# Four more w_out tiles summed on TensorE, and a newly searched order, in an attention-plus-FFN kernel

## The chip, the cores and the metric

The kernel runs on one core of a Trainium2 chip. The metric is the device time of one launch in microseconds; three runs of the kernel before gave a median of 753.57 us. Engines are called PE (TensorE matmul, PEld its weight loads), DVE (VectorE), ACT (ScalarE), POOL (GpSimd) and SP (SyncE, which issues most DMAs).

## The reference

Block-causal attention over 8 batches, 8 heads, 576 positions and 64 channels per head (blocks of 64 positions), whose output is the input of a gated feed-forward layer. The weights `w_in`, `conv_w` and `w_out` arrive as float64.

```python
scores = q @ k.T / 8;  scores[block_i < block_j] = -1e9
x = softmax(scores) @ v                      # (8, 576, 512) over heads
h = maximum(x @ w_in, 0)                     # 512 -> 1024
conv_out[t] = sum_k conv_w[k] * h[t + k - 1] # 3 taps along the sequence
out = (h * sigmoid(conv_out)) @ w_out        # 1024 -> 512
```

## The kernel before

Matmuls run in fp32r, and precision is kept by splitting each operand in a high part and a low part (`hi`, `lo`), so that a product is three matmuls: in L1872 `wih`x`x`, `wil`x`x` and `wih`x`x` low (x @ w_in), and in L1938 `woh`x`gh`, `wol`x`gh`, `woh`x`gl` (the second product of the layer). A pair of heads is a visit: scores (L1475, L1477, L1428), maximum and exponential (L1485, L1488), normalizing on POOL (L1399), transposes (L1670), product with v (L1790). The first batch is done in two parts, A (positions 0 to 255, lines L1331, L1583, L1609, L1766) and B (the rest, lines L1522, L1541, L1424), so that the feed-forward work starts early. After every fourth visit `ffn` adds two halves of the feed-forward layer of a batch.

The weights are decoded from float64 during the first batch, in 16 tiles of 128 x 512 numbers: `load_w_in` for tiles f = 0 to 7 (through the buffers `gh`, `gl`, named by tile parity) and `load_w_out` for f = 8 to 15 (raw words in `x`, scratch in `stage`). Both call `split`, whose steps are: a DMA (L1147 or L1173); `decode` with ACT Abs (L1018), a clamp (L1024, on POOL for every tile but the first), three DVE integer steps (L1029, L1041, L1045) and a DVE product that gives the remainder of the word (L1052). Then there are two ways:

- Where f is not in `WPE` (`whole`), POOL adds the remainder to the main part (L1056), ACT rounds that to `hi` (L1087), and POOL subtracts `hi` to give `lo` (L1090).
- Where f is in `WPE`, ACT rounds the main part to `hi`, DVE writes the remainder into `lo`, PE forms `lo` minus `hi` in a PSUM bank with two 512-column matmuls (L1103 with `nident`, L1106 with `rident`), and DVE adds the main part and writes `lo` (L1109).

The order of the instructions is not that of the code. Each step is recorded with an engine, a guessed duration, its dependences and buffers, and `Plan.order` lays them out: from the numbers in `TARGETS` (one due time for each step) and the guessed durations it simulates the five engines and writes out each engine's queue. The engines then run their queues strictly in that order, and wait on semaphores. The planner puts filler matmuls (L2090, on `blank` or `rident`, 512 columns, result unused) into PE's queue wherever its own simulation leaves PE idle for more than 0.4 us; how many, comes out of its guess. For DMAs it keeps one running time `moved` for the transfers: each transfer begins at the later of `moved` and 1.2 us after its issue, and takes `xfer`, times 1.5 as long as `moved` is under a limit.

Of the kernel before, what the change touches and what calls it, by code (L numbers as in the profile page):

```python
# [18 lines left out]
PE, DVE, ACT, POOL, SP = 0, 1, 2, 3, 4  # L19

TARGETS = """
# [299 lines left out]
class Plan:  # L321
# [53 lines left out]
    def order(self, targets, skip, fill, clock, pair):  # L375
# [76 lines left out]
        moved = 0.0  # L452
        done = []
        left = len(self.ops)
        while left:
            left -= 1
            best = None
            for e in range(5):
                t = free[e]
                if e == PE:  # L460
# [3 lines left out]
                    for o in open_:  # L464
                        at, need = vacant(o, t)
# [4 lines left out]
                        at = max(at, rtime[o.seq])  # L470
# [1656 lines left out]
```

## Time and profile before

| | |
|---|---|
| median of 3 runs | 753.57 us (753.52 to 753.73) |
| the profiled execution | 753.84 us, its span 752.1 us |
| PE busy | 743.1 us, 5169 matmuls |
| DVE, ACT, POOL busy | 623.4, 603.7, 435.9 us |
| granted TensorE clock | 1.000 |

The span runs from the first to the last instruction; the 1.7 us beside it lie around the program. A busy PE is not PE at its peak: an isolated matmul also counts for the time in which its weights are loaded and its result drains, and the filler matmuls count too. "idle before" is the time in which the engine had nothing to do ahead of a group of instructions, and what ended that. The chain is the sequence of work that ended last, followed back from the last instruction.

### The profile page before, as it was taken

How to read it: one execution, taken by the hardware profiler on the slowest of the kernel's cores; microseconds unless marked ns; L12 is line 12 of the kernel's file. 1: busy time of each engine (PE TensorE's matmuls, PEld its weight loads, DVE VectorE, ACT ScalarE, POOL GpSimd, SP SyncE). 2: the span in 40 equal slices, each digit the busy share in tenths (PEclk: the TensorE clock that was granted, in tenths of full speed). 3: DMA queues.
4: the chain of work that ended last, by engine and by line, in shares of the span. 5: the costliest groups of instructions: out<-in, count | busy, mean ns of one | idle time of the engine just before them, and what ended most of it. 6: DMA issues, size and time to landing. Idle time of an engine off the chain costs nothing.

```text
span 752.1 us, 16813 instructions
## 1 busy us (share of the span) xinstructions
PE 743.1 (99%) x5169; PEld 668.6 (89%) x5169; DVE 623.4 (83%) x1836; ACT 603.7 (80%) x1754; POOL 435.9 (58%) x650
## 2 busy tenths in 40 slices
PE   8999999999999999999999999999999999999998
PEld 5567899889899898999989899998989889898997
DVE  6998999999989698898979789898988779896541
ACT  5989989778988687887979679797978769786752
POOL 2557678656666457475665547566566555565421
PEclk9999999999999999999999999999999999999999
DMA  9763857566553546655462655544565445430001
GB/s 264 183 167 104 192 119 165 120 158 158 129 135 91 132 106 145 145 125 134 102 149 70 158 130 128 142 107 117 126 137 127 110 122 134 118 78 15 15 28 43
DMA packets 165628, 92.63 MB, mean 123 GB/s; under 512 B 134924, under 2 KB 142116, under 8 KB 165540
## 3 DMA queue, kind: packets, MB, share of 16 engines
q1 hardware_dynamic: 164996, 91.43, 50.0%
q8 instruction: 42, 0.69, 0.4%
q14 instruction: 46, 0.38, 0.2%
q10 hardware_dynamic: 544, 0.13, 0.1%
HBM read 38.30 MB, written 9.44 MB: 63 GB/s over the span
## 4 chain that ended last, share of the span: by engine, by line
PE 85%; ACT 5%; DMA 3%; DVE 3%; POOL 2%; SPq 2%; issue 1%; ACTq 0%; POOLq 0%
PE bank L1938 26%; PE bank L1872 25%; PE bank L1790 11%; PE bank L1670 7%; PE bank L1477 4%; PE bank L1475 4%; PE bank L1428 3%; PE bank L1221 2%; DMA qkf<-in_k_dram 1%; PE bank L1766 1%; DMA vn<-in_v_dram 1%; ACT p4f L1444 1%; DMA x<-in_moe_w_out_dram 1%; DMA qnf<-in_k_dram 0%; DVE st L1485 0%
## 5 line engine op out<-in xcount | busy, mean ns | idle before, releaser
L1872 PE MATMUL bank<-x,wih 128*128 128x290 f32 (+3 forms) x1024 | 199.6, 300 | 0.1
L1912 POOL TENSOR_TENSOR gl<-t,gh 128x289 fp32r<-128x289 f32 (+3 forms) x128 | 103.7, 815 | 101.7 <-ACT gh L1909 96.7
L1872 PEld LDWEIGHTS bank<-x,wih 128*128 128x128 f32 x1024 | 157.0, 189 | 3.2 <-ACT p3f L1488 0.3
L1938 PE MATMUL bank<-woh,gh 128*128 128x512 f32 (+1 forms) x296 | 118.5, 400 | 0.0
L1938 PE MATMUL bank<-wol,gh 128*128 128x512 f32 (+1 forms) x296 | 115.0, 388 | 0.0
L1938 PE MATMUL bank<-woh,gl 128*128 128x512 f32 (+1 forms) x296 | 114.9, 388 | 0.0
L1872 PE MATMUL bank<-x,wil 128*128 128x290 f32 (+3 forms) x512 | 111.1, 298 | 0.0
L1485 DVE TENSOR_REDUCE st<-bank 128x1 f32<-128x128 f32 (+1 forms) x224 | 107.3, 483 | 2.9
L1684 DVE TENSOR_TENSOR ptbl<-bank,ptbh 128x512 fp32r<-128x512 f32 (+1 forms) x142 | 89.3, 632 | 4.5 <-ACT ptbh L1681 1.9
L1681 ACT ACTIVATE ptbh<-bank 128x512 fp32r<-128x512 f32 (+2 forms) x180 | 87.4, 502 | 6.8 <-PE bank L1670 5.8
L1893 DVE SCALAR_TENSOR_TENSOR t<-bank,cw,t 128x289 f32<-128x289 f32 (+3 forms) x128 | 64.7, 505 | 23.1 <-ACT t L1889 21.3
L1872 PEld LDWEIGHTS bank<-x,wil 128*128 128x128 f32 x512 | 82.3, 188 | 0.6
L840 POOL TENSOR_SCALAR vv<-vn 128x320 fp32r<-128x320 f32 (+2 forms) x62 | 28.0, 453 | 88.1 <-PE bank L1790 37.0
L1477 PE MATMUL bank<-kl,qz 128*128 128x128 f32 (+1 forms) x224 | 71.7, 322 | 0.0
L1938 PEld LDWEIGHTS bank<-woh,gl 128*128 128x128 f32 x296 | 55.5, 188 | 12.6
L1889 ACT ACTIVATE t<-bank,cw 128x289 f32<-128x289 f32 (+3 forms) x128 | 64.2, 502 | 2.3
L1897 DVE SCALAR_TENSOR_TENSOR t<-bank,cw,t 128x288 f32<-128x288 f32 (+3 forms) x128 | 64.7, 506 | 1.1
L1813 DVE TENSOR_TENSOR xt<-bank,xt 64x256 f32<-64x256 f32 x112 | 51.5, 460 | 16.0 <-ACT xt L1810 13.0
L1790 PE MATMUL bank<-ptbl,vv 128*64 128x192 f32 x240 | 64.6, 314 | 0.0
L1902 ACT ACTIVATE t<-t 128x289 f32<-128x289 f32 (+3 forms) x128 | 56.9, 445 | 7.0 <-DVE t L1897 6.1
L1909 ACT ACTIVATE gh<-t 128x289 fp32r<-128x289 f32 (+3 forms) x128 | 56.1, 444 | 7.4 <-DVE t L1905 6.7
L1905 DVE SCALAR_TENSOR_TENSOR t<-t,bank 128x289 f32<-128x289 f32 (+3 forms) x128 | 57.0, 447 | 5.0 <-ACT t L1902 4.1
(186 smaller groups left out, 2009.2 us busy)
## 6 DMA issues: line engine op xcount, KB each, us to landing
out_dram<-stage SPq DMA_DIRECT2D x35, 256.0 KB, 2.2
ka<-kh SPq DMA_DIRECT2D x56, 144.0 KB, 2.6
kb<-kh SPq DMA_DIRECT2D x56, 144.0 KB, 2.6
vn<-in_v_dram SPq DMA_DIRECT2D x60, 128.0 KB, 2.7
qnf<-in_q_dram SPq DMA_DIRECT2D x56, 128.0 KB, 2.4
knf<-in_k_dram SPq DMA_DIRECT2D x56, 128.0 KB, 2.7
x<-in_moe_w_out_dram SPq DMA_DIRECT2D x8, 512.0 KB, 4.8
qz<-qh SPq DMA_DIRECT2D x28, 144.0 KB, 2.5
```

Source lines behind the costliest of these rows:

```text
L1477: nc.tensor.matmul(sb.ap[:, 0:nk], qz.ap[:, z:z + 128], kl.ap[:, 0:nk], start=False, stop=True)
L1485: nc.vector.tensor_reduce(out=st.ap[:, i:i + 1], in_=sb.ap[:, 0:nk], op=ALU.max, axis=AX.X, negate=True)
L1681: nc.scalar.activation(out=hi(), in_=src(), func=AF.Copy)
L1684: nc.vector.tensor_tensor(out=lo(), in0=src(), in1=hi(), op=ALU.subtract)
L1790: nc.tensor.matmul(tb.ap[0:m, q0 - qa:qb - qa], vv.ap[:, chunk(c), w[ps_]], pm.ap[:, 128 * c + q0:128 * c + qb] if qa == 0 else pm.ap[:, c ...
L1872: nc.tensor.matmul(fb.ap[:, 0:n2], wt[:, c, fs], xs[c][xi].ap[:, x0:x0 + n2], start=(n + c - c0 == 0), stop=(n + c - c0 == 3 * NCC - 1))
L1889: nc.scalar.activation(out=t.ap[:, 0:no], in_=fb.ap[:, own:own + no], func=AF.Copy, scale=cw[:, NFC + f:NFC + f + 1])
L1893: nc.vector.scalar_tensor_tensor(out=t.ap[:, i0:no], in0=fb.ap[:, own + i0 - 1:own + no - 1], scalar=cw[:, f:f + 1], in1=t.ap[:, i0:no], o ...
L1897: nc.vector.scalar_tensor_tensor(out=t.ap[:, 0:i1], in0=fb.ap[:, own + 1:own + 1 + i1], scalar=cw[:, 2 * NFC + f:2 * NFC + f + 1], in1=t.a ...
L1905: nc.vector.scalar_tensor_tensor(out=t.ap[:, 0:no], in0=t.ap[:, 0:no], scalar=1.0, in1=fb.ap[:, own:own + no], op0=ALU.add, op1=ALU.mult)
L1912: nc.gpsimd.tensor_tensor(out=gbuf[1].ap[:, f, carry:carry + no], in0=t.ap[:, 0:no], in1=gbuf[0].ap[:, f, carry:carry + no], op=ALU.subtract)
L1938: nc.tensor.matmul(fb.ap[:, 0:cut], gbuf[a].ap[:, f, cs], w[:, f, ds], start=(f == 0 and n == 0), stop=(f == NFC - 1 and n == 2))
```

## The change

Three things are edited. `WPE` takes in the four w_out tiles that were left out (f = 9, 11, 13, 15), so that all 16 weight tiles go the second way. The planner's price of transfers is changed in two places: the limit under which a transfer takes 1.5 times as long goes from 4.5 to 8.5 us, and the transfer of a v tile goes from 0.8 to 1.5 us. And all the numbers in `TARGETS` are others, found by a new search, so every engine's queue is in another order from the first instructions on.

```diff
 TARGETS = """
-242 286 317 355 385 418 264 296 365 340 443 409 460 486 708 703 273 378 423 422 441 482 495 520 534 541 415 421 419 426 634 594 433 456 482 496 494 483 501
...
+213 152 338 292 386 451 201 231 335 331 431 412 398 340 749 696 120 185 245 198 282 248 281 294 300 357 316 355 348 355 558 558 406 384 411 393 409 426 498
...
@@ -545,7 +545,7 @@
             if e == SP:
 
                 o.end = max(o.end, moved - 4.4)
-                moved = max(o.end + 1.2, moved) + o.xfer * (1.5 if moved < 4.5 else 1.0)
+                moved = max(o.end + 1.2, moved) + o.xfer * (1.5 if moved < 8.5 else 1.0)
                 o.lat = moved + 0.4 - o.end
@@ -652,7 +652,7 @@
     EA = True
-    WPE = tuple(range(8)) + (8, 10, 12, 14)
+    WPE = tuple(range(16))
     WPA = ()
@@ -898,7 +898,7 @@
-        ld = pl.op(SP, 2.4, go, at if load_at is None else load_at, bufs=[vn], xfer=0.8)
+        ld = pl.op(SP, 2.4, go, at if load_at is None else load_at, bufs=[vn], xfer=1.5)
```

Counted over the whole program, PE gets 8 more real matmuls of 512 columns (L1103 and L1106, 4 to 8 each on `woh` and `wol`), DVE 4 more instructions (L1109), POOL 8 fewer (4 of L1056, 4 of L1090); ACT and SP have the same instructions in another order. There are 38 fillers in both: 18 on `blank` and 20 on `rident` before, 19 and 19 now.

POOL's queue around the second w_out tile, where the first batch's scores of part B are normalized (`p2f`, `p3f`). Before:

```order
L1559 TENSOR_SCALAR p3f_105<-p3f_105,st_145 128x512
L1056 TENSOR_TENSOR stage<-stage,x 128x512
L1559 TENSOR_SCALAR p2f_99<-p2f_99,st_147 128x384
L1024 TENSOR_SCALAR stage<-stage 128x512
L1090 TENSOR_TENSOR wol<-stage,woh 128x512
L1559 TENSOR_SCALAR p2f_101<-p2f_101,st_147 128x384
L1912 TENSOR_TENSOR gl<-t,gh 128x255
```

Now:

```order
L1559 TENSOR_SCALAR p3f_105<-p3f_105,st_145 128x512
L1559 TENSOR_SCALAR p2f_99<-p2f_99,st_147 128x384
L1559 TENSOR_SCALAR p2f_101<-p2f_101,st_147 128x384
L1024 TENSOR_SCALAR stage<-stage 128x512
L1559 TENSOR_SCALAR p3f_103<-p3f_103,st_147 128x512
L1559 TENSOR_SCALAR p3f_105<-p3f_105,st_147 128x512
L1912 TENSOR_TENSOR gl<-t,gh 128x255
```

Two 512-column POOL instructions between the normalizing steps are gone, and the clamp L1024 of the tile stands behind two of those steps.

PE's queue at the last fillers, in part A of the first batch (`qkr` are q and k to be transposed, `p0r`, `p1r` the exponentials, `ptah`, `ptal` their transposes). Before, where the last filler is the one after `wih`:

```order
L2090 MATMUL bank<-rident 128x512 x4
L1766 MATMUL bank<-ptal,ptbl 64x256
L1766 MATMUL bank<-ptal,ptbl 64x128
L2090 MATMUL bank<-rident 128x512 x3
L1670 MATMUL bank<-rident,p0r_92 128x128
L1670 MATMUL bank<-rident,p1r_96 128x128 x2
L2090 MATMUL bank<-rident 128x512
...
L1103 MATMUL bank<-wih,nident 128x512
L2090 MATMUL bank<-rident 128x512
```

Now, where the last are the three ahead of `qkr_118`:

```order
L2090 MATMUL bank<-rident 128x512
L1670 MATMUL bank<-rident,p0r_94 128x128
L1670 MATMUL bank<-rident,p1r_98 128x128 x2
L1766 MATMUL bank<-ptah,ptbl 64x256
L1766 MATMUL bank<-ptah,ptbl 64x128
L1331 MATMUL bank<-rident,qkr_124 128x128 x4
L2090 MATMUL bank<-rident 128x512 x3
L1331 MATMUL bank<-rident,qkr_118 128x128 x4
```

The fillers now end earlier in the work: ahead of the last one stood 78 real matmuls before, and 45 now.

SP's queue of loads at the start (`gh`, `gl` are w_in tiles, `x` a w_out tile, `t` conv_w, `qkf` q and k of part A). Before:

```order
L1147 DMA gh_184<-in_moe_w_in_dram 128x4x256
L1147 DMA gl_186<-in_moe_w_in_dram 128x4x256
L1147 DMA gh_184<-in_moe_w_in_dram 128x2x256
L957 DMA qkf00_113<-in_q_dram 128x2x64
L1189 DMA t_191<-in_moe_conv_w_dram 24x256
...
L1147 DMA gl_186<-in_moe_w_in_dram 128x4x256
L957 DMA qkf01_115<-in_q_dram 128x2x64
```

Now:

```order
L1147 DMA gh_185<-in_moe_w_in_dram 128x4x256
L1189 DMA t_187<-in_moe_conv_w_dram 24x256
L1147 DMA gl_189<-in_moe_w_in_dram 128x4x256
L1147 DMA gh_185<-in_moe_w_in_dram 128x2x256
L957 DMA qkf00_113<-in_q_dram 128x2x64 x2
L1147 DMA gl_189<-in_moe_w_in_dram 128x4x256
L1173 DMA x_143<-in_moe_w_out_dram 128x1024
L957 DMA qkf01_115<-in_q_dram 128x2x64
```

conv_w moves to second place, and the first w_out tile comes ahead of the second pair of heads (`qkf01`), where it came in 13th place before.

434 rows, old and new, of the table TARGETS are left out of this document.

## The prediction

> **What bounds the kernel now.** I read first the page's busy times and its chain, then busy time by stretches, then the waits, and last the groups of the instructions that change.
>
> ```profile
> span 752.1 us, 16813 instructions
> PE 743.1 (99%) x5169; PEld 668.6 (89%) x5169; DVE 623.4 (83%) x1836; ACT 603.7 (80%) x1754; POOL 435.9 (58%) x650
> PE 85%; ACT 5%; DMA 3%; DVE 3%; POOL 2%; SPq 2%; issue 1%; ACTq 0%; POOLq 0%
> ```
>
> PE is busy for all but 9.0 us, and 85% of the chain is PE's. The other 15% (113 us) is where an order can win or lose. The next view (stretches of the span; columns: length, then busy us and instructions of each engine, granted clock, DMA) shows where those lie.
>
> ```profile
> 0.00:8.00 8.00, 6.89 (x18) 5.11 (x18) 1.98 (x11) 3.12 (x6) 1.70 (x8) 1.00 0.80 237
> 8.00:20.00 12.00, 10.15 (x70) 6.98 (x70) 11.58 (x34) 8.57 (x27) 4.25 (x8) 1.00 1.14 287
> 20.00:30.00 10.00, 9.19 (x57) 5.94 (x54) 9.17 (x27) 9.32 (x31) 5.49 (x9) 1.00 0.85 213
> 30.00:40.00 10.00, 9.04 (x53) 5.71 (x53) 9.50 (x23) 9.54 (x30) 4.30 (x10) 1.00 0.48 125
> 40.00:50.00 10.00, 10.00 (x73) 7.76 (x72) 9.47 (x27) 7.93 (x26) 6.21 (x7) 1.00 0.69 184
> 50.00:60.00 10.00, 9.28 (x52) 5.71 (x51) 9.23 (x25) 9.45 (x27) 6.48 (x10) 1.00 0.45 123
> 60.00:80.00 20.00, 20.00 (x147) 15.79 (x146) 16.04 (x41) 19.51 (x56) 12.40 (x20) 1.00 0.45 119
> 80.00:100.00 20.00, 19.89 (x134) 16.94 (x135) 18.71 (x53) 17.98 (x54) 15.18 (x22) 1.00 0.70 162
> 200.00:700.00 500.00, 500.00 (x3557) 462.76 (x3556) 423.31 (x1268) 405.02 (x1184) 296.94 (x445) 1.00 0.49 119
> ```
>
> From 200 us on PE never stops, and DVE has 15% to spare: there no order wins much, and any matmul added costs its full time. Up to 60 us it is otherwise. DVE and ACT are at 92 to 97% in most stretches, and PE's idle time sums, after the first 8 us, to 1.85 + 0.81 + 0.96 + 0 + 0.72 = 4.3 us. In those 60 us PE also runs its fillers, which are no work:
>
> ```profile
> L2090 PE MATMUL bank<-blank 128*128 128x512 f32 x18 | 6.9, 562 | 1.1 <-DVE blank L834 1.1
> L2090 PE MATMUL bank<-rident 128*128 128x512 f32 x20 | 6.7, 424 | 0.3 <-ACT qa L845 0.3
> ```
>
> So 13.6 us of fillers and 4.3 us of idle time stand in the first 60 us: a start that is limited by the loads and by DVE and ACT. What PE waited for there, and which waits a load ended (engine, line, what ended it: us, times, longest):
>
> ```profile
> PE bank L1103 <- ACT wih L1087: 0.8, 2, 0.5
> PE bank L1766 <- ACT ptah L845: 0.7, 2, 0.4
> PE bank L1670 <- POOL p1f L1624: 0.6, 2, 0.4
> PE bank L1424 <- ACT ptbh L845: 0.5, 1, 0.5
> ...
> ACT gh L1018 <- DMA gh<-in_moe_w_in_dram: 1.9, 1, 1.9
> ACT gl L1018 <- DMA gl<-in_moe_w_in_dram: 1.2, 1, 1.2
> ACT stage L1018 <- DMA x<-in_moe_w_out_dram: 1.2, 1, 1.2
> ```
>
> PE is held by ACT above all, and ACT by loads three times. The chain of waits shows the third one with its consequence (start, us, what), and two later places:
>
> ```profile
> 45.75 3.93 DMA x<-in_moe_w_out_dram
> 49.70 0.05 ACT stage L1018
> ...
> 53.10 0.75 PE bank L1424 x2
> ...
> 82.99 1.30 POOL stage L1056
> 84.32 0.63 ACT woh L1087
> ...
> 94.01 2.06 DMA vn<-in_v_dram
> ```
>
> ACT's queue stood until 49.7 us for a w_out tile that took 3.93 us to land, and PE's next score matmul (L1424) waited behind it. Later a POOL sum that the change removes is on the chain (1.30 us), and then a v tile (2.06 us), whose price the change raises.
>
> **The change part by part.** The groups (line, engine, operation, form, count | busy, mean ns | idle before):
>
> ```profile
> L1103 PE MATMUL bank<-woh,nident 128*128 128x512 f32 x4 | 1.7, 414 | 0.0
> L1106 PE MATMUL bank<-wol,rident 128*128 128x512 f32 x4 | 1.8, 461 | 0.1
> L1109 DVE TENSOR_TENSOR wol<-bank,stage 128x512 fp32r<-128x512 f32 x4 | 2.7, 679 | 0.0
> L1056 POOL TENSOR_TENSOR stage<-stage,x 128x512 f32<-128x512 f32 x4 | 5.2, 1305 | 5.9 <-DVE x L1052 4.0 <-DVE st L1548 1.8
> L1090 POOL TENSOR_TENSOR wol<-stage,woh 128x512 fp32r<-128x512 f32 x4 | 5.1, 1282 | 1.3 <-ACT woh L1087 1.3
> ...
> 708.15 11.20 PE bank L1938 x48
> ```
>
> *PE, eight matmuls more.* Their means of 414 and 461 ns run from issue to the modelled end and overlap their neighbours. In a stream, 48 matmuls of 512 columns took 11.20 us on the chain, 233 ns each. Eight cost 8 x 0.233 = 1.9 us. Ends: 0, if all fall into idle time of the start, and 3.5 us at the means (4 x 0.414 + 4 x 0.461). I take 1.9, since the tiles stand at 40 to 110 us, where PE is busy nearly without a break.
>
> *Fillers.* One more on `blank`, one fewer on `rident`. The extra one runs before the first decoded tile is there: the first L1103 waited for ACT behind all 18. Cost 0; if that cover were gone, 0.23.
>
> *DVE, four L1109 more.* 4 x 0.679 = 2.7 us. From 40 to 100 us DVE is idle for 0.53 + 0.77 + 3.96 + 1.29 = 6.6 us, so that there is room, and the next stage has more. I take 0; the ends are 0 and +2.7, if DVE has no gap where these fall.
>
> DVE's step on the raw w_out words may get cheaper when POOL is quieter (duration ns min/median/max):
>
> ```profile
> L1041 DVE SCALAR_TENSOR_TENSOR stage<-x,stage x8: 673/732/1007, 20.0 to 98.8; 128x512 int32<-128x512 int32 x8
> ```
>
> The Trainium skill (SBUF — State Buffer, on the shared port pair) says that a DVE operation with two SBUF inputs and a GpSimd operation that reads SBUF exclude each other, and the second to come stands still until the first is done. The spread from 673 to 1007 ns agrees with that without showing its cause. By that rule, the sum would be lower by up to 8 x (732 - 673) ns = 0.5 us of DVE's time, which is hidden like the 2.7 us.
>
> *POOL, eight fewer.* 4 x 1.305 + 4 x 1.282 = 10.3 us go from an engine that is 62 to 76% busy there. Nobody on PE waits for these by the trace; ACT's L1087 does, once on the chain. A tile of the second way needs no L1056 ahead of L1087. I take -0.4; ends 0 and -1.3, the one sum on the chain. What is late next at that place is `p4f`, which had the exponentials of part B to wait for anyway.
>
> *The new order and the new prices.* This is the largest term, and the trace of before cannot show it. The order in front of the reader has its fillers behind 45 real matmuls instead of 78: with slower loads assumed, the planner puts its empty time in the beginning and then has PE fed. The w_out tiles' loads stand further ahead of their use (the first moves past the loads of the second pair of heads, which are then later by its transfer; conv_w past two w_in tiles). The steps of the loads move past each other in SP's queue alone; POOL issues none. What such an order can win at most is the idle time and the `rident` fillers after 8 us, 4.3 + 6.7 = 11 us; what it can lose is as much idle time again, 4.3 us. I take the idle time from 20 to 60 us, 0.81 + 0.96 + 0.72 = 2.5 us, and ACT's wait for the w_out tile, 1.2 us, which it handed on to PE: -3.7. The first two ACT waits on loads stay: the first tile is still the first load. The number is nearer to the small end because DVE and ACT, at 92 to 97%, can't deliver much sooner.
>
> Sum against the profiled execution's 753.84 us: +1.9 + 0 + 0 - 0.4 - 3.7 = -2.2, 751.6 us. The median of the runs is 0.27 us below that execution, so 751.4 us.
>
> **The rivals.**
>
> *The waits only move (no change).* DVE and ACT set the pace of the start, and an order doesn't make them faster. For it: 11.58 of 12 us DVE busy at 8 to 20 us, 9.5 of 10 after that. Against it: ACT falls to 7.93 at 40 to 50 us, just where it stands for a load. Then the order wins no more than the w_out wait and the POOL sum, 1.2 + 0.4, against 1.9: 753.57 + 0.3 = 753.9 us.
>
> *DVE becomes the bound (slower).* Place: 40 to 100 us. The four L1109 lie in front of the maxima (L1538, L1431) that ACT and then PE need. Price: 2.7 us on top of PE's 1.9, with the 1.6 us of the rival above won: 753.57 + 2.7 + 1.9 - 1.6 = 756.6 us. It decides once DVE is over 95% busy in the whole stretch of 40 to 100 us; before, it had 80% at 60 to 80 us, which speaks against it.
>
> *The loads are priced too late (slower).* A filler that the planner puts in runs whether the data is there or not. The new queue has one run of eight on `rident`; if the data is there when it begins, PE loses 8 x 0.233 = 1.9 us, and with the 1.9 of the added matmuls and 1.6 won the time is 755.8 us. Against it: the start's loads took long in the trace of before too.
>
> ```profile
> 1.27 5.34 DMA qkf<-in_k_dram
> 7.04 2.66 DMA qkf<-in_q_dram
> 14.26 3.72 DMA qnf<-in_k_dram
> ```
>
> **How the numbers follow.** My forecast has 0.44, the waits that only move 0.29, DVE as the bound 0.17, loads priced too late 0.10. A measurement of this kernel can tell 0.2% (1.5 us) from no change. The first is faster by about that much and more, so faster 0.44, same 0.29, slower 0.27. The likeliest case alone spans 749.2 (753.57 + 1.9 - 0.4, less the 4.3 us of idle time after 8 us and 1.6 us of fillers) to 752.0 (where the order wins 3.1 us in place of 3.7). The range for 8 in 10 takes in the no-change case and the two slower ones: 749.0 to 756.6 us.
>
> **What would show it.** In the profile after: PE with 8 more matmuls and some 1.9 us more of work; L1109 at 8 on `wol`; L1056 and L1090 gone from the w_out tiles and POOL at about 426 us. If I am right, PE idles under 2 us from 20 to 60 us, and ACT has no wait for a w_out load over 0.5 us. If DVE is the bound, its stretches from 40 to 100 us are over 95%, and PE waits for maxima. If loads are priced too late, the run of eight fillers ends well after the landing of its q and k. What would make it wrong beside these is the late part: if PE's waits after 200 us, now 0, come to microseconds because the new order has another engine late there, or if the last tiles, which the order mixes more closely with the last x @ w_in matmuls, wait for ACT, DVE and POOL at the end.

## The result and the profile after

The changed kernel took 757.71 us (757.28 to 758.90, three runs): 4.14 us more, a ratio of 1.0055 with a 95% interval of 1.0040 to 1.0070. The prediction was 751.4 us, 749.0 to 756.6. The profiled execution took 757.71 us, its span is 755.9 us.

The page of the changed kernel, span, busy times and chain:

```profile
span 755.9 us, 16813 instructions
PE 745.6 (99%) x5177; PEld 669.5 (89%) x5177; DVE 629.5 (83%) x1840; ACT 605.3 (80%) x1754; POOL 426.8 (56%) x642
PE 85%; DVE 6%; ACT 5%; DMA 2%; issue 1%; POOL 0%; SPq 0%; ACTq 0%; DVEq 0%
```

PE has 2.5 us more of busy time and 1.3 us more outside it. On the chain POOL and SP's queue fall from 2% each to 0% and DVE doubles, from 3 to 6%. By stretches (columns as before):

```profile
0.00:8.00 8.00, 6.24 (x19) 4.69 (x19) 2.63 (x15) 3.04 (x7) 1.32 (x7) 1.00 0.75 218
8.00:20.00 12.00, 9.65 (x55) 6.51 (x56) 10.15 (x29) 7.53 (x23) 3.72 (x5) 1.00 1.01 274
20.00:30.00 10.00, 9.08 (x66) 6.10 (x65) 9.18 (x28) 8.83 (x30) 4.62 (x10) 1.00 0.86 210
30.00:40.00 10.00, 9.49 (x59) 6.15 (x59) 9.50 (x27) 9.90 (x33) 4.45 (x10) 1.00 0.45 115
40.00:50.00 10.00, 9.99 (x68) 7.26 (x69) 9.56 (x25) 9.63 (x28) 6.19 (x8) 1.00 0.55 138
50.00:60.00 10.00, 9.79 (x55) 6.22 (x54) 9.46 (x24) 7.70 (x22) 3.58 (x5) 1.00 0.70 182
60.00:80.00 20.00, 19.61 (x138) 15.43 (x137) 17.37 (x43) 19.05 (x55) 11.54 (x19) 1.00 0.38 114
80.00:100.00 20.00, 19.77 (x130) 16.30 (x130) 18.79 (x55) 18.35 (x54) 11.77 (x18) 1.00 0.74 177
200.00:700.00 500.00, 499.55 (x3546) 461.57 (x3545) 428.68 (x1277) 407.00 (x1189) 297.93 (x445) 1.00 0.50 119
```

From 20 to 60 us PE idles 0.92 + 0.51 + 0.01 + 0.21 = 1.65 us, against 2.49 before: what the prediction hoped for came. But from 0 to 20 us it idles 4.11 us instead of 2.96, and 8 to 20 us holds 55 matmuls instead of 70. The last row matters most: in the same 500 us PE runs 3546 matmuls instead of 3557, and DVE is busy for 5.4 us more, in a stretch that has none of the added instructions. DVE's instructions haven't become longer: over the whole program their durations sum to 704.8 us before and 707.5 after, and the 2.7 us are the four L1109. In the stretch, 9 more of them fall (1277 against 1268), and neighbours overlap less in the trace (sum of durations less busy time: 52.5 us before, 50.0 after).

Two waits of the first 60 us, and the groups of the change, in the changed kernel:

```profile
PE bank L1331 <- DMA qkf<-in_k_dram: 0.9, 1, 0.9
...
ACT stage L1018 <- DMA x<-in_moe_w_out_dram: 0.4, 1, 0.4
```

```profile
L1103 PE MATMUL bank<-woh,nident 128*128 128x512 f32 x8 | 3.8, 475 | 0.3 <-DVE t L1905 0.2
L1106 PE MATMUL bank<-wol,rident 128*128 128x512 f32 x8 | 3.3, 410 | 0.0
L1109 DVE TENSOR_TENSOR wol<-bank,stage 128x512 fp32r<-128x512 f32 x8 | 5.4, 679 | 0.2 <-PE bank L1106 0.2
```

PE now waits for k of part A (L1331), which it did not before; ACT's wait for a w_out tile is down from 1.2 to 0.4 us.

**Where the time is lost, by the starts of the matmuls.** "Busy" doesn't tell what a matmul's wait inside the pipeline costs, so I took every start of a PE matmul from the trace and the gap to the next start. What a gap after a matmul of a line and shape needs, I took from the kernel before: the lower quartile of such gaps (for L1331, L1424 and the matmuls of part A's and B's scores, which start in pairs, the mean). The rest is called lost; a filler's gap is lost as a whole. Needed time is 692.60 us before and 694.65 after, 2.05 us more for the eight matmuls. Lost time by stretch, in us:

| kernel | 0-20 | 20-60 | 60-200 | 200-700 |
|---|---|---|---|---|
| before | 12.38 | 10.08 | 11.45 | 20.62 |
| after | 13.80 | 8.57 | 11.24 | 22.79 |
| e1_plus8 | 12.40 | 9.58 | 10.87 | 20.49 |
| e2_plus8dve4 | 12.39 | 9.57 | 11.82 | 20.63 |
| e3_minus8dve4 | 13.83 | 7.68 | 12.36 | 22.75 |
| h1_early_before_late_after | 12.32 | 10.15 | 10.65 | 22.46 |
| h2_early_after_late_before | 13.90 | 8.41 | 11.63 | 20.81 |
| w16_before_table | 12.40 | 10.19 | 11.84 | 20.49 |
| d_before | 12.19 | 10.17 | 12.22 | 20.36 |
| d_after | 14.18 | 8.66 | 11.13 | 20.52 |

After against before: 2.05 needed, +1.42 and -1.51 at the start, -0.21, then +2.17 from 200 us on: 3.9 us, of a span that is 3.8 us longer. The start wins nothing, and the long even part loses. Each row is one execution, but the last column repeats over the runs. Counted once more with the lower quartile for all shapes of that stretch (its levels are then some 1.5 us higher), eight traces with the old due times there lose 21.9 to 22.4 us and eight with the new ones 24.0 to 24.7; the ninth with the new ones is d_after, below, at 22.1.

### The profile page after: what moved, and what is told of

Read it like the earlier page. It is cut to its first block, busy times and chain, and to the rows that moved or that the text cites. A ratio compares the mean times of both kernels' runs of the same rounds, so it can differ in the third digit from the quotient of the medians.

```text
span 755.9 us, 16813 instructions
## 1 busy us (share of the span) xinstructions
PE 745.6 (99%) x5177; PEld 669.5 (89%) x5177; DVE 629.5 (83%) x1840; ACT 605.3 (80%) x1754; POOL 426.8 (56%) x642
## 4 chain that ended last, share of the span: by engine, by line
PE 85%; DVE 6%; ACT 5%; DMA 2%; issue 1%; POOL 0%; SPq 0%; ACTq 0%; DVEq 0%
PE bank L1872 25%; PE bank L1938 25%; PE bank L1790 11%; PE bank L1670 7%; PE bank L1477 4%; PE bank L1475 4%; PE bank L1428 3%; PE bank L1221 2%; PE bank L1766 1%; DMA x<-in_moe_w_out_dram 1%; DVE st L1485 1%; DMA qkf<-in_k_dram 1%; DVE ptbl L1684 1%; PE bank L1522 1%; DVE xt L1813 1%
## 5 line engine op out<-in xcount | busy, mean ns | idle before, releaser
L1872 PE MATMUL bank<-x,wih 128*128 128x290 f32 (+3 forms) x1024 | 196.8, 300 | 0.0
L1485 DVE TENSOR_REDUCE st<-bank 128x1 f32<-128x128 f32 (+2 forms) x224 | 106.3, 481 | 2.7
L1684 DVE TENSOR_TENSOR ptbl<-bank,ptbh 128x512 fp32r<-128x512 f32 (+1 forms) x142 | 89.1, 632 | 10.7 <-ACT ptbh L1681 8.0
L1681 ACT ACTIVATE ptbh<-bank 128x384 fp32r<-128x384 f32 (+2 forms) x180 | 87.6, 504 | 11.2 <-PE bank L1670 10.6
L1477 PE MATMUL bank<-kl,qz 128*128 128x128 f32 (+3 forms) x224 | 71.3, 322 | 0.0
L1897 DVE SCALAR_TENSOR_TENSOR t<-bank,cw,t 128x288 f32<-128x288 f32 (+3 forms) x128 | 64.6, 507 | 1.5
L1886 ACT ACTIVATE bank<-bank 128x290 f32<-128x290 f32 (+3 forms) x128 | 51.6, 404 | 16.7 <-PE bank L1872 16.1
```

The lines of the kernel that those rows point to most:

```text
L1477: nc.tensor.matmul(sb.ap[:, 0:nk], qz.ap[:, z:z + 128], kl.ap[:, 0:nk], start=False, stop=True)
L1485: nc.vector.tensor_reduce(out=st.ap[:, i:i + 1], in_=sb.ap[:, 0:nk], op=ALU.max, axis=AX.X, negate=True)
L1681: nc.scalar.activation(out=hi(), in_=src(), func=AF.Copy)
L1684: nc.vector.tensor_tensor(out=lo(), in0=src(), in1=hi(), op=ALU.subtract)
L1872: nc.tensor.matmul(fb.ap[:, 0:n2], wt[:, c, fs], xs[c][xi].ap[:, x0:x0 + n2], start=(n + c - c0 == 0), stop=(n + c - c0 == 3 * NCC - 1))
L1897: nc.vector.scalar_tensor_tensor(out=t.ap[:, 0:i1], in0=fb.ap[:, own + 1:own + 1 + i1], scalar=cw[:, 2 * NFC + f:2 * NFC + f + 1], in1=t.a ...
```

## The experiments

The theories. **1**: the eight matmuls cost their full time. **2**: DVE's four L1109 make DVE late, and PE with it. **3**: the new order as such costs some 2 us, whatever work is added; **3a** in its late part, **3b** in its start (loads, idle time, clock). The medians, with that of the kernel before on the same chip; the ratio is that of the comparison's runs taken together, so that it can differ from the medians' by some 0.05%:

| run | us (lowest to highest) | before | ratio, 95% |
|---|---|---|---|
| e1_plus8 | 754.96 (754.20-755.62) | 754.06 | 1.0007, 0.9998-1.0016 |
| e2_plus8dve4 | 755.75 (755.29-756.70) | 754.06 | 1.0020, 1.0011-1.0028 |
| e3_minus8dve4 | 757.50 (755.92-758.59) | 754.06 | 1.0040, 1.0026-1.0054 |
| e4_nodve4 | 757.16 (756.48-758.50) | 754.06 | 1.0036, 1.0024-1.0049 |
| a0_after | 758.07 (756.63-759.36) | 753.61 | 1.0058, 1.0046-1.0070 |
| h1_early_before_late_after | 754.97 (754.44-755.35) | 753.61 | 1.0017, 1.0009-1.0026 |
| h2_early_after_late_before | 756.15 (755.93-757.07) | 753.61 | 1.0037, 1.0024-1.0049 |
| h5_before_newprice | 755.73 (755.36-757.81) | 753.61 | 1.0032, 1.0019-1.0044 |
| h6_after_oldprice | 759.42 (757.45-762.82) | 754.36 | 1.0070, 1.0050-1.0090 |
| h9_wout_later | 760.77 (759.93-763.46) | 754.36 | 1.0092, 1.0075-1.0108 |
| d_before | 753.41 (752.38-754.25) | 754.36 | 0.9983, 0.9973-0.9994 |
| d_after | 755.06 (753.91-757.37) | 754.36 | 1.0012, 1.0003-1.0021 |
| w16_before_table | 756.41 (756.08-757.45) | 753.68 | 1.0041, 1.0029-1.0054 |
| f1_after_fill | 758.11 (757.51-759.03) | 753.68 | 1.0060, 1.0048-1.0072 |
| f2_before_nofill | 756.85 (756.35-759.72) | 753.68 | 1.0052, 1.0039-1.0066 |

### The added work, in a fixed order

e1_plus8, the kernel before with eight matmuls more, at the even w_out tiles (the change adds its own at the odd ones):

```diff
         def less():
+            for _ in range(2 if f in (8, 10, 12, 14) else 0):
+                nc.tensor.matmul(view(), nident, hi, start=True, stop=True)
             nc.tensor.matmul(view(), nident, hi, start=True, stop=False)
```

> The kernel before, every queue in its order; only the four even w_out tiles run L1103 three times instead of once (8 matmuls of 512 columns more, the same result). Theory 1 (the added matmuls cost their full time on PE, 8 x 0.233 us): +1.9, about 755.4 us. Theory 2 (DVE's four added L1109 are what made PE late) and theory 3 (the new order as such costs some 2 us, whatever work is added) say nothing else of this run. If the matmuls fall into idle time of PE: 753.6.

Measured +0.9 us by the medians, +0.5 by the ratio (-0.2 to +1.2): theory 1's 1.9 is excluded for these places, where the matmuls are half hidden. The table of lost time shows why: 0.5 us of the matmuls' time came out of what PE lost anyway from 20 to 60 us, 0.6 us out of 60 to 200.

e2_plus8dve4, with DVE's work as well (`f in (8, 10, 12, 14)`, L1109 twice):

```diff
         def fl2():
-            nc.vector.tensor_tensor(out=lo, in0=view(), in1=src(), op=ALU.add)
+            for _ in range(2 if f in (8, 10, 12, 14) else 1):
+                nc.vector.tensor_tensor(out=lo, in0=view(), in1=src(), op=ALU.add)
```

> The kernel before, every queue in its order; the four even w_out tiles run L1103 three times and L1109 twice, so PE and DVE have the work that the change adds to them, at other tiles. Theory 2: 4 x 0.679 = 2.7 us of DVE come on top of the matmuls' 1.9, up to 758.2 us, and anyway over 756.5. Theory 3: DVE's part is hidden, 755.4 us as with the matmuls alone.

+1.7 us: DVE's 2.7 us cost 0.8 more (755.75 against 754.96), in the trace all at 60 to 200 us (lost time 11.82 against 10.87), nothing later. Not hidden, as theory 3 had it, and not enough for theory 2.

e3_minus8dve4 and e4_nodve4, the changed kernel in its order, without L1103, L1106 and L1109 of the odd w_out tiles, or without L1109 alone (these lines stand at the head of each step that is left out):

```diff
+            if f in (9, 11, 13, 15):
+                return
```

> The changed kernel, every queue in its order, but the odd w_out tiles leave out L1103, L1106 and L1109 (their low parts lack the rounding error of the high part); the work that the change added to PE and DVE is gone, the new order stays. Theory 3: 757.7 - 1.9 = 755.8 us, still about 2 us over the kernel before. Theory 2: 757.7 - 1.9 - 2 to 2.7, 753.1 to 753.8 us.

> The changed kernel, every queue in its order, but the odd w_out tiles leave out L1109 alone (2.7 us less on DVE; their low parts lack the rounding error of the high part); PE's added matmuls stay. Theory 2: 755.0 to 755.8 us. Theory 3: 757.7 us, within 0.5.

757.50 and 757.16 us, still 3.4 and 3.1 us over the kernel before: with the added work gone again most of the loss stays, and the lost time from 200 us on is the changed kernel's (22.75). That is against theory 2. The medians hold executions at a granted clock of 0.998, of which below; those of e3 at 1.000 took 755.92 and 756.73 us, 2.3 us over the kernel before, as theory 3 had it (755.8).

### The early and the late order apart

The changed kernel once more, a0_after:

> The changed kernel once more, beside the three below. 757.3 to 758.9 us as before. If the granted clock of some executions is 0.998 again, these are about 1.5 us slower than those at 1.000.

758.07 us, 4.5 us over the kernel before; four of six executions at 0.998 or less (758.01 to 759.36), two at 1.000 (756.63, 757.76). By the medians of the two groups that is 0.9 us, less than the 1.5 expected. The two hybrids take the due times of each step from one table or the other, by whether the step was due before 180 us in the kernel before. By the planner's clock, the queues of PE and DVE in h1 are those of the kernel before up to 168 us and those of the changed kernel from 204 us on, but for the last steps; in h2 it is the other way round, with the seam from 171 to 198 us. The rule in short (the edits themselves exchange numbers of `TARGETS`):

```python
# h1: WPE and prices of before; h2: WPE and prices of the change
target = due_before if (due_before < 180 us) == (kernel is h1) else due_after
```

> The kernel before with its own instructions and order up to about 168 us, and from about 202 us on the order of the changed kernel (the due times of steps that are due after 180 us are taken from the changed kernel). None of the added matmuls, DVE instructions or prices is in it. Theory 3a (the order after 200 us costs 2.1 us of small waits on DVE and ACT): the kernel before + 2.1, 755.7 to 756.4 us, and PE's matmuls from 200 us on take as much longer. Theory 3b (the start sets it: loads of q and k that come late, PE at rest for too long): no loss, 753.5 to 754.2. Theory 2: no loss, since DVE has nothing more to do.

> The changed kernel (all 16 tiles on TensorE, the new prices) with its order up to about 171 us, and from about 198 us on the order of the kernel before. Theory 3a: the changed kernel - 2.1, 755.2 to 755.8 us at a clock of 1.000. Theory 3b: 757.3 us or more. Theory 2: as 3b, since the added DVE work stands in the start and all of it is still there. If some executions show a clock of 0.998, the start is what brings that about; if none, the late order.

The late order alone costs 1.4 us (754.97 against 753.61; by the ratio 0.7 to 2.0), and taking it back wins 1.9 us (756.15 against 758.07). Part of the 1.9 is the clock, since four of the six executions of a0 were at 0.998 or less and one of the five of h2; among executions at 0.999 or over the means are 756.3 us (h2) and 757.2 us (a0), 0.9 apart. So the late order costs some 1 to 2 us by the times and 1.8 to 2.0 by the lost time of the traces. Both medians stay outside the times given for theory 3a, which had 2.1; its sign and its place hold in both directions, and theories 2 and 3b gave no loss in h1. No execution of h1 is below 0.999 and one of h2 is at 0.998: the lower clock goes with the changed start. The same stretch in h1 and in h2:

```profile
200.00:700.00 500.00, 499.58 (x3551) 462.00 (x3550) 426.74 (x1272) 405.50 (x1185) 296.89 (x445) 1.00 0.50 119
```

```profile
200.00:700.00 500.00, 499.94 (x3553) 462.50 (x3552) 423.69 (x1271) 404.79 (x1186) 298.21 (x446) 1.00 0.50 119
```

DVE's busy time goes with the order: 426.7 us with the late order of the change, 423.7 with that of before, which had 423.3. The lost time is 22.46 and 20.81. What remains of the change in h2, 2.5 us, is its start with the added work and the seam.

### Which engine is late after 200 us

For each gap in 200 to 700 us more than 40 ns over the median of its pair of lines and shapes, I took the last semaphore that PE waited for there and the engine that gave it (us):

| | DVE | ACT | POOL | all, the unassigned too |
|---|---|---|---|---|
| before | 1.6 | 1.5 | 1.2 | 7.8 |
| after | 3.4 | 2.4 | 0.7 | 9.9 |
| h1 | 3.5 | 2.2 | 0.7 | 9.8 |
| h2 | 1.7 | 1.4 | 1.1 | 7.9 |
| d_before | 1.8 | 1.4 | 1.0 | 7.6 |
| d_after | 2.5 | 1.2 | 0.6 | 7.9 |

The table doesn't ask how long ago that semaphore came. Counting only those that came after the start of the matmul before, or up to 0.2 us ahead of it, DVE has 0.5 us before, 1.6 after, 1.8 in h1, 0.6 in h2, 0.8 in d_before and 0.7 in d_after, and most of the rest has no engine. Of the 1.6, 1.0 ends with L1684, DVE's subtraction that gives the low part of the transposed exponentials (`ptal`, `ptbl`); it has 0.3 before. These waits are short, and the view of waits, which lists those from 0.2 us up, has one of them (L1670 for `ptal`, 0.2 us, after). To see whether they are the cause, d_before and d_after leave out one tap of the convolution on DVE (L1897) from the second batch on:

```diff
             def c2b(fb=fb, t=t, f=f):
+                if b:
+                    return
                 nc.vector.scalar_tensor_tensor(out=t.ap[:, 0:i1], ...
```

> The kernel before without L1897 (one tap of the convolution, some 0.5 us each on DVE) from the second batch on, every queue otherwise in its order: DVE has 57 us less to do after 100 us. PE's matmuls are all there. What it gains is what PE waits for DVE late in the program, directly or through ACT. Theory 3a: 1 to 1.5 us faster than the kernel before (its waits on DVE after 200 us come to 1.6 us).

> The changed kernel without L1897 from the second batch on, as in the run beside it. Theory 3a, with DVE as the engine that is late in the new order (3.4 us of PE's waits after 200 us end with DVE, 1.6 before): 2.5 to 3.5 us faster than the changed kernel, so that the distance between the two kernels without L1897 is 2.0 to 3.0 us instead of 4.1 to 4.5. If the late loss is in PE's own order and not in DVE: the distance stays 4 us or more.

The kernel before gains 0.95 us. The changed one gains 3.0 beside 758.07 on another chip, or 3.8 if each is taken against the kernel before on its own chip (+4.46 and +0.70). The two are 1.65 us apart instead of 4.1 to 4.5, under what was expected. The stretch in d_before, then in d_after:

```profile
200.00:700.00 500.00, 499.70 (x3556) 463.05 (x3555) 391.08 (x1180) 404.44 (x1186) 298.45 (x445) 1.00 0.50 119
```

```profile
200.00:700.00 500.00, 499.81 (x3563) 463.68 (x3562) 396.54 (x1190) 407.38 (x1193) 298.89 (x446) 1.00 0.50 120
```

With 32 us taken off DVE the late order loses hardly more than the old one (20.52 and 20.36 us). So the late loss isn't in PE's own order: it is DVE's lateness, directly or through the chain of ACT and DVE steps that L1897 stands in. Which of the two, and which of DVE's late instructions stand wrongly, was not tried; the waits point at L1684.

### The start: loads, prices, the way of the tiles

h9_wout_later moves one load in SP's queue of the changed kernel:

```diff
+    x = next(o for o in sp if 'load_w_out' in o.fn.__qualname__)
+    queue.remove(x)
+    queue.insert(queue.index(sp[sp.index(x) + 9]) + 1, x)
```

> The changed kernel, every queue in its order but for one load: the first w_out tile's (512 KB) is moved nine loads back in SP's queue, behind the loads of q and k of the second pair of heads. Theory 3b (in the new start this load makes q and k late, they land at 11.8 to 12.6 us instead of 10.2 to 10.9, and PE has nothing to do from 8 to 20 us): 1 to 1.7 us faster than the changed kernel, 756.0 to 757.0 us, q and k landed before 11.3 us, and no clock below 0.999. Theory 3a (only the late order costs): within 0.5 us of the changed kernel's 757.8.

q and k landed at 10.0 to 11.0 us as wanted, but the kernel is 6.4 us over the one before, 2 us worse than the change. The waits from 12 to 24 us in h9:

```profile
PEld bank L1331 <- ACT p0f L1609: 2.8, 1, 2.8
PE bank L1331 <- ACT p0f L1609: 2.6, 1, 2.6
ACT stage L1018 <- DMA x<-in_moe_w_out_dram: 2.1, 1, 2.1
```

ACT's queue is strict: its step on the w_out tile stands ahead of the next exponential, ACT waits 2.1 us for the load, and PE 2.6 us for that exponential. So this run can't tell what the late q and k of the changed kernel cost (PE waits 0.9 us for k there); it shows that nine places back is too far for this load, and no place between was tried. And it did more (h9, stretches of 2 us):

```profile
16.00:18.00 2.00, 0.35 (x3) 0.14 (x1) 1.38 (x3) 0.08 (x1) 0.00 (x0) 1.00 1.06 314
18.00:20.00 2.00, 0.86 (x3) 0.41 (x3) 1.04 (x5) 2.00 (x7) 0.62 (x1) 1.00 0.99 282
20.00:22.00 2.00, 1.95 (x14) 1.51 (x15) 1.45 (x4) 1.19 (x2) 1.92 (x3) 0.71 0.60 151
22.00:24.00 2.00, 1.85 (x7) 0.98 (x7) 2.00 (x6) 0.40 (x2) 1.18 (x3) 0.50 0.79 239
```

After 4 us in which PE worked 1.2, its granted clock fell to a half (third column from the right: 0.71, 0.50). That is the 0.997 of this execution; the other four of h9 show 0.993 to 0.998.

The price edits alone in the kernel before (h5), and undone in the changed one (h6, the same lines the other way round):

```diff
-                moved = max(o.end + 1.2, moved) + o.xfer * (1.5 if moved < 4.5 else 1.0)
+                moved = max(o.end + 1.2, moved) + o.xfer * (1.5 if moved < 8.5 else 1.0)
-        ld = pl.op(SP, 2.4, go, at if load_at is None else load_at, bufs=[vn], xfer=0.8)
+        ld = pl.op(SP, 2.4, go, at if load_at is None else load_at, bufs=[vn], xfer=1.5)
```

> The kernel before with the two edits of the transfer prices alone (the due times and the way of the tiles as before), so that the order moves where the planner now believes loads to come later. If the new prices are nearer to the chip, this is no slower than before: 753.0 to 754.3 us. If they make the planner wait for loads that are there already (theory 3b): over 754.8 us.

> The changed kernel with the two edits of the transfer prices undone and its own due times kept, so that the planner lays it out anew. If due times fit only the prices they were searched with (theory 3: each table is worth what its own layout is worth), it is no faster than the changed kernel, 757.5 us or more. If the new prices as such are worse than the old (the kernel before lost 2.1 us by them alone), 755.5 to 756.5 us.

+2.1 us in the one; 759.42 us in the other, 5.1 us over the kernel before on its chip, where the change has 4.5. The first mixture is slower than the table with its own prices, the second no faster. So neither price shows itself the better. That due times fit only the layout that they were searched with agrees with both runs; no run shows it by itself.

The way of the tiles alone, w16_before_table, with the old prices and the due times of the kernel before (those of the four tiles' steps and some of the start shifted):

```diff
-    WPE = tuple(range(8)) + (8, 10, 12, 14)
+    WPE = tuple(range(16))
```

> The headline edit alone: all 16 tiles summed on TensorE, the old transfer prices, and the due times of the kernel before (those of the four tiles' own steps and some of the start shifted by up to a few us, so that the planner finds places for them). POOL's eight instructions are gone. Theory 1 with full cost: the kernel before + 1.9 to 2.0, about 756 us. If part of it falls into waits of PE, as when the same matmuls (+0.9) or matmuls and DVE work (+1.7) were added in the old order: + 0.9 to + 1.7. If POOL's relief gives something back: under + 0.9.

+2.7 us, more than every expectation: PE's needed work is up as in the change, and at 20 to 200 us it loses 0.5 us more than before (22.03 against 21.53). Of POOL's relief nothing is seen.

### The clock

f1_after_fill, the changed kernel with more fillers, and f2_before_nofill, the kernel before without those on `rident`; both edit `work`, which writes a run of k fillers:

```diff
         fills.append(k)
+        k += {2: 1, 3: 4, 4: 1}.get(len(fills), 0)
```

> The changed kernel, every queue in its order, with six fillers more in the gaps that PE has from 9 to 13 us (runs of 3, 1 and 1 become 4, 5 and 2). Clock theory (PE rests too much there, so that in some executions its clock is halved for some 3 us, which costs 1.5 us): no execution below 0.999, and a median of 757.0 to 757.8 us, at or under the fast executions of the changed kernel. If the fillers only delay what stands behind them: 6 x 0.233 = 1.4 us more than those, 758.5 us or over.

```diff
         fills.append(k)
+        k = k if len(fills) == 1 else 0
```

> The kernel before, every queue in its order, without any of its 20 fillers on rident (the 18 on blank stay). Clock theory: PE rests in the start as it does in the changed one and more, most executions show a clock of 0.998 or less, with time lost: 755 to 757.5 us. If the clock does not hang on them: all at 1.000 and no slower than the kernel before, 753 to 754.3 us.

The clock came as expected: with six fillers more, all five executions at 1.000; without the 20 on `rident`, all six of the kernel before at 0.986 to 0.993, and 3.2 us slower. Of 71 executions of the kernel before, one was below 0.999. Five executions are few, since the changed kernel had two of six at 1.000 without these fillers. The time came only in f2. f1 is no faster than the changed kernel (4.43 us over the kernel before on its own chip, against 4.46). It is 0.9 us slower than the mean of a0's two executions at 1.000, so that the fillers seem to cost about what the clock gave back. The profiled execution of d_after, which has the changed start, was one at 0.998:

```profile
8.00:10.00 2.00, 1.76 (x7) 0.86 (x5) 1.61 (x5) 1.22 (x3) 1.02 (x2) 1.00 1.04 343
10.00:12.00 2.00, 1.08 (x6) 0.60 (x5) 2.00 (x7) 0.95 (x3) 0.03 (x1) 1.00 1.03 222
12.00:14.00 2.00, 1.85 (x12) 1.33 (x14) 1.46 (x4) 1.40 (x4) 0.31 (x1) 0.87 0.45 131
14.00:16.00 2.00, 2.00 (x10) 1.44 (x9) 0.95 (x3) 0.42 (x3) 0.30 (x1) 0.50 1.15 303
16.00:18.00 2.00, 2.00 (x8) 1.60 (x8) 1.78 (x5) 1.94 (x9) 0.42 (x1) 0.78 1.15 252
```

(0.13 x 2 + 0.50 x 2 + 0.22 x 2) / 0.5 = 3.4 us at half speed. That the clock goes by windows of 3.4 us and knows a half and a whole is in the Trainium skill (TensorE: Matmul & The Clock Gate, "What's actually happening"), and the trace agrees (in f2 the stretches of one clock last 3.41 or 6.83 us). The same page ("Why this matters for your kernels") warns of idle gaps over some 3 us; here the clock fell at some 13.5 us with PE recorded busy for 1.08 and 1.85 of the 2 us in the two stretches up to 14 us, and no two matmul starts from 8 us on were further apart than 1.03 us. The measurement decides: a window need not be empty. Where the windows lie may be why only some executions lose the clock. Counted in steps of 3.41 us back from the fall, d_after has a window from 10.07 to 13.48 us with PE busy for 2.34 us. In the profiled execution of the changed kernel, whose clock stayed at 1.000, the same count from its first clock record gives 8.00 to 11.42 and 11.42 to 14.83 us, with 2.54 and 2.79. No run tests this, and busy time alone doesn't settle it: h6 kept its clock after 2.19 us from 5.60 to 9.01.

No version that computes the whole reference was faster than the kernel before; d_before, the only faster one, leaves out work.

## Why the prediction was wrong, point by point

- **PE, +1.9.** Needed time rose by 2.05 us, as worked out. In a fixed order 0.5 to 0.9 us of it reached the end (e1). In w16, laid out anew with the odd tiles, nothing of it was hidden. So the size is right for one layout and twice too big for the other, and the reason "PE is busy nearly without a break" was too strong for e1's.
- **Fillers, 0.** One more on `blank`, one fewer on `rident`, as said; nothing shows a cost of that. By the starts in the traces, 102 real matmuls stand ahead of the last filler before and 55 now, not 78 and 45; that they end earlier holds.
- **DVE, cost 0.** Mis-sized: 0.8 us (e2), inside its ends of 0 and 2.7. DVE's gaps from 60 to 100 us (3.96 + 1.29) did not take all of it: the loss is in the trace from 60 to 200 us.
- **POOL, -0.4.** Not seen: w16 has the relief and gains nothing. The page has POOL at 426.8 us, as promised. L1041 on `stage`, with the two-input step, became evener (its longest 1007 ns before, 850 after), which agrees with the shared-port rule of the Trainium skill (SBUF — State Buffer, "Who interferes with whom"). But w16, with the same eight POOL instructions gone, still has three of its eight at 980 to 1100 ns: the evenness came with the new start, not with the relief as such, and its 0.5 us would be hidden.
- **The new order, -3.7.** This step failed. Its signs came (PE's idle time at 20 to 60 us 1.65 us, under 2; ACT's wait for a w_out tile 0.4 us, under 0.5), but the idle time had moved to the first 20 us: +1.42 and -1.51 of lost time, a gain of 0.1 in place of 3.7. And the late part lost some 1 to 2 us (h1, h2; 2.2 in the traces), where the prediction gave nothing.
- **The reading behind it.** "From 200 us on PE never stops: there no order wins much" was read from 500.00 busy of 500.00. In that stretch 20.6 us are lost between the starts of matmuls, more than the 12.4 of the first 20 us. The busy column can't show it. The last sentence of the prediction named the late part as what could make it wrong, but gave it no term and no chance.
- **The rivals.** DVE as the bound named the engine, but the wrong place: at 40 to 100 us DVE is at 96, 95, 87 and 94%, not over 95% in all of it, and most of what PE loses to DVE is lost after 200 us. The waits only moving is what the start did. Loads priced too late: the sign came, since the last of the run of eight fillers starts at 16.26 us, and q and k of the pair behind them had landed by 12.80. Its price did not, as the timeline of the changed kernel's PE (start, length, what) shows.

```profile
14.65 2.00 PE L2090 MATMUL bank<-rident 128*128 128x512 f32 x8
16.49 0.28 PE L1331 MATMUL bank<-rident,qkr 128*128 128x128 f32 x2
17.24 0.36 PE L1331 MATMUL bank<-rident,qkr 128*128 128x128 f32 x2 [0.47 <-ACT p0f L1609]
```

Two of the four matmuls behind it stood 0.47 us more for ACT, so that for them the fillers cost nothing. What they cost the other two was not tried.

The 4.1 to 4.5 us, as far as the runs split them: 1 to 2 us late order; 2.5 us start with the added work (h2). How much of the 2.5 is the new start stays open: the added work alone costs 1.7 us in the old order (e2), and 2.7 where the planner lays it out with the old due times (w16), which leaves nothing. The new start also loses the clock for 3.4 us in some executions. What that adds to the median isn't settled: f1 kept the clock and was not faster.

## What to carry to other kernels

A busy engine at 100% is no proof that an order can't lose there: count the instructions in equal stretches, or the gaps between starts, before and after. Don't expect an order that was searched under one set of prices to hold its worth under another; test an edit in a fixed order first, and splice two orders in time to find where one loses. A load moved for the sake of one queue must be followed to the in-order engine that waits for it next.

## What the runs showed of the hardware

PE's clock is nearer its edge in a start limited by loads than the mean of 1.000 tells: without fillers it fell in six of six executions of the kernel before, with fewer matmuls at 8 to 20 us (55 in place of 70) in four of six of the changed one. A filler of 512 columns, 233 ns from start to start at full clock, was 427 and 426 ns apart in the halved stretch of d_after (15.78, 16.20, 16.63 us). In h9 one late load cost PE twice: 2.6 us of waiting behind ACT, and then 3.4 us at half clock.
